# Seven block products instead of eight in more chunks of a MoE layer, behind attention

## The chip, the cores and the metric

The kernel runs on one core of a Trainium2 chip. The metric is the device time of one execution in microseconds (us). Engines are named as in the profile: PE (TensorE: matmuls; PEld its weight loads), DVE (VectorE), ACT (ScalarE), POOL (GpSimd), SP (SyncE, which issues all DMAs here).

## The reference: what is computed

Eight batches of eight heads of causal attention with a decay, 576 tokens and 64 features a head; the result, 4608 tokens of 512 features, goes through a two-layer network (called MoE here, though there is one expert) with 2048 hidden features and the activation mish:

```python
scores = scale * np.matmul(q, k.transpose(0, 1, 3, 2))
decay = cum[:, :, :, None] - cum[:, :, None, :]      # cum: running sum of log(f)
scores = np.where(causal, -1e9, scores + decay)
attn = softmax(scores)                               # over the keys
x = np.matmul(attn, v)                               # -> 4608 x 512
h = x @ w_in                                         # 512 -> 2048
g = h * np.tanh(np.log1p(np.exp(h)))                 # mish
out = g @ w_out                                      # 2048 -> 512
```

All inputs and outputs are float32. The kernel keeps the precision by splitting each float32 operand into two float16 parts, hi and lo, and adding three products: hi·hi, hi·lo and lo·hi.

## The kernel before, in words

**Attention** runs in 32 groups (batch b, pair of heads p; g = 4b + p). A group's queries and keys come in as `qk32`, are split into `hl`, and moved by DMA into `ST1` and `ST2`; scores go to PSUM banks 0 to 3, a DVE pass adds the mask and finds the row's minimum, ACT takes the exponential into `st` (the spare tile `ST1[2]`) or `more_e`, ACT and DVE split it into the two halves of an `hb` tile, and a DMA transpose turns that into `pt` for the product with v (`vv`). The result `x` (tokens on partitions) is split into `xp` and turned by a DMA transpose into `xa`: features on partitions, 512 tokens of one batch in the columns. The last 64 tokens of all batches collect in `xat`.

**The MoE layers** run in nine chunks of 512 tokens: chunk c < 8 is the first 512 tokens of batch c and reads `xa[c % 2]`; chunk 8 is `xat`. The hidden features go in 16 blocks of 128, j = 0 to 15. The first layer (`m1_items`) adds 4 blocks of inputs with 3 products each, 12 matmuls of 128x128 by 128x512, in a PSUM bank; ACT applies mish into a `me` tile; `halves` rounds it to `gh` (ACT or DVE) and takes the rest `gl` (DVE). The second layer (`m2_items`) makes 12 matmuls a block into banks 4 to 7. In chunks 1 to 8 four blocks of the first layer (`GJ = 4`) alternate with the same four of the second; such a half is a phase, and the phases also group the activations, since mish and the exponential need different tables on ACT. Chunk c's work is recorded interleaved with the attention of batch c + 1, so chunks 7 and 8 have no attention left beside them.

**Seven products.** In chunks 7 and 8 seven pairs of feature blocks (`TWINS`) are done as a 2x2 block product in the Winograd form: two feature blocks by two halves of the 512 inputs on the weight's side, two halves of the inputs by two halves of 256 tokens on the other. `diffs_of` builds four sums and differences of weight blocks, `sums_of` four of the chunk's token blocks, in float32 and split into hi and lo again; `m1_seven` makes seven products of 6 matmuls with 256 columns each in place of eight, in three PSUM banks, and puts the results together with adds into `me`.

**Order.** The program records every instruction with the tiles it touches and its cost by a table, and a planner (`Program.schedule`) makes a list schedule forward and backward several times and emits the instructions in the planned order; on the chip each engine then takes its own list in order, with semaphores between the engines. Tiles come from rings (`Ring.tile`): `tag` names the ring, `bufs` its length, and an instruction that writes a ring's tile waits for the last reader of the buffer's former content. `nc.choose` lets the planner pick the engine. Names in the tables below: `b` is a PSUM bank, `mn` a group's row minima, `wall` all weights as hi and lo, `v` and `vv` the values, `cinv` and `gsc` scales.

Of the kernel before, what the change touches and what calls it, by code (L numbers as in the profile page):

```python
# [58 lines left out]
NME = 5  # L59
NOT = 2  # L60
NGH = 10
GJ = 4
NEX = 2
# [19 lines left out]
NQK = 2  # L83
NX = 1
# [26 lines left out]
TB = "2,4,6,8,10,13,16,19"  # L111
# [13 lines left out]
NV = 6  # L125
# [6 lines left out]
PRIO = 200  # L132
C7 = 7
PLAIN = 0
TWINS = [(0, 1), (2, 3), (4, 5), (6, 7), (8, 9), (10, 11), (13, 14)]
# [442 lines left out]
def attn_moe(ctx: ExitStack, tc: tile.TileContext, qk, v, f, w_in, w_out, out):  # L578
# [78 lines left out]
    xat = xa[2]  # L657

# [275 lines left out]
    def load_qk(g):  # L934
        b, p = divmod(g, NP)
        if g in (2, 3):
# [86 lines left out]
    sel = more_e.rearrange("p a n -> p (a n)").bitcast(F16)[:, 0 : 9 * P].rearrange("p (t k) -> p t k", t=9)  # L1023
# [6 lines left out]
    def max_items(g):  # L1030
# [5 lines left out]
        def begin():  # L1036

            s["mx"] = sp.tile([P, 20], F32, name=f"mx{g}", tag="mx", bufs=4)
            nc.gpsimd.memset(s["mx"][:, 0:8:4], -3e38)
# [354 lines left out]
    def x_items(g):  # L1394
# [29 lines left out]
        return [(parts, 60), (turn, 60), (turn_tail, 60)]  # L1424
# [41 lines left out]
    twin_of = {a: b for a, b in TWINS}  # L1466
    diffs, sums = {}, {}
# [4 lines left out]
    def sums_of(c):  # L1472
        t = xa[c % 2] if c < B else xat
        if c < B:
            halves = [flat16(xa[1 - c % 2])[:, 2048 * d : 2048 * d + 2048] for d in range(2)]
            homes = [(x[:, 0:1024], x[:, 1024:2048]) for x in halves]
        else:
            v = sp.tiles["v32"]
            homes = [[v[2 * d + k].bitcast(F16)[:, 0:1024] for k in range(2)] for d in range(2)]
        spare = [x[:, 0:CH] for x in sp.tiles["pt"] + sp.tiles["x32"]]  # L1480
        for d in range(2):
            ga, gb, f1, f2 = spare[4 * d : 4 * d + 4]
            hi, lo = homes[d]
            sums[c, d] = [x.rearrange("p (k n) -> p k n", k=4) for x in (hi, lo)]
            for g, dt in ((ga, d), (gb, d + 2)):
                nc.choose(*([(e, "tensor_tensor", (), dict(out=g, in0=t[:, dt, 0], in1=t[:, dt, 1], op=ALU.add))]
                    for e in ("vector", "gpsimd")))
            n1, n2 = slice(0, 256), slice(256, CH)
            tt = nc.vector.tensor_tensor
            tt(out=f1[:, n1], in0=ga[:, n2], in1=ga[:, n1], op=ALU.subtract)  # L1490
            tt(out=f1[:, n2], in0=gb[:, n2], in1=ga[:, n2], op=ALU.subtract)
            tt(out=f2[:, n1], in0=f1[:, n2], in1=ga[:, n1], op=ALU.add)
            tt(out=f2[:, n2], in0=gb[:, n1], in1=f2[:, n1], op=ALU.subtract)
            split(hi, lo, (f1, f2))

    def split(hi, lo, fs):
        for k, f in enumerate(fs):
            w = slice(CH * k, CH * k + CH)
            nc.choose(*(scaled(hi[:, w], f, None, e) for e in ("scalar", "vector")))
            nc.choose(*(sub(lo[:, w], f, hi[:, w], e) for e in ("vector", "gpsimd")))  # L1500

    def diffs_of(a):
        k = [x for x, _ in TWINS].index(a)
        home = flat16((sp.tiles["qk32"] + sp.tiles["hl"] + ST2 + ST1)[k])
        hi, lo = home[:, 0:1024], home[:, 1024:2048]
        w1, w2 = (wall[:, place[0, j]] for j in (a, twin_of[a]))
        fa, fb = (more_e[:, k] for k in range(2))
        s1, s2 = (x[:, 0:CH] for x in sp.tiles["v32"][4:6])
        diffs[a] = [x.rearrange("p (k n) -> p k n", k=4) for x in (hi, lo)]
        for f, w in ((fa, w1), (fb, w2)):  # L1510
# [363 lines left out]
```

## Time and profile before

| what | value |
|---|---|
| median of 3 runs | 1040.64 us (1037.7 to 1042.4) |
| the profiled execution | 1045.19 us, of which the span from the first to the last instruction is 1043.5 us |
| mean granted PE clock | 0.989 |
| DMA | 140.44 MB, mean 135 GB/s |

The page of a profile gives, for each engine, its busy time, share of the span and number of instructions; then 40 slices of the span, in which a digit is a tenth of busy time (PEclk: of granted clock); then the chain of work that ended last; then groups of equal instructions with their total busy time, the mean of one in ns, and the idle time of the engine just before them with what ended it. Every instruction of the program is recorded through one line of a helper, so the rows have one line number (L311) and are told apart by their tiles: `me<-b,cinv` is the mish that reads a PSUM bank and writes `me`. A matmul's length in the records includes its latency; two in a row overlap, so a rate is read from a run of them.

### The profile page before, as it was taken

The page shows a single profiled execution, that of the slowest core. Times are in us where ns is not written, and L with a number is a line of the kernel's source. Part 1 is how long each engine was busy: PE and PEld are TensorE (multiplying, and loading weights), DVE is VectorE, ACT ScalarE, POOL GpSimd, SP SyncE. Part 2 cuts the span into 40 slices and gives each one's busy share as a digit, 9 for nine tenths or more (in the row PEclk, how much of TensorE's full clock was granted, in tenths as well). Part 3 has the DMA queues.
Part 4 walks back from the last instruction along what each step waited for, and adds up shares of the span by engine and source line. Part 5 has one row for each costly group of instructions (what it writes and reads, how often), then busy time and mean ns, then how long its engine had stood idle before and what let it go on. Part 6 is the DMA issues. An engine that isn't in the chain of part 4 may idle for free.

```text
span 1043.5 us, 20548 instructions
## 1 busy us (share of the span) xinstructions
PE 998.4 (96%) x7638; PEld 557.7 (53%) x7638; DVE 739.6 (71%) x2043; ACT 703.1 (67%) x1309; POOL 13.0 (1%) x73
## 2 busy tenths in 40 slices
PE   2899999999999999999999999999999999999998
PEld 1687565544454544455555445454544545656664
DVE  8777788997777677776766767777676559962432
ACT  6565698987777867776777776778677675443322
POOL 1000001000000000000000000000000000000000
PEclk9898999999999999999999999999999999999999
DMA  7857737399776966776676776766557423001001
GB/s 216 257 177 220 230 92 204 88 212 238 176 144 138 202 135 132 158 163 145 147 148 153 169 148 135 153 158 134 116 125 144 86 56 80 15 4 41 1 1 41
DMA packets 245409, 140.44 MB, mean 135 GB/s; under 512 B 213436, under 2 KB 214012, under 8 KB 245308
## 3 DMA queue, kind: packets, MB, share of 16 engines
q1 hardware_dynamic: 245308, 139.12, 57.7%
q8 instruction: 60, 0.98, 0.4%
q14 instruction: 41, 0.34, 0.1%
HBM read 47.78 MB, written 11.76 MB: 57 GB/s over the span
## 4 chain that ended last, share of the span: by engine, by line
PE 62%; DVE 14%; ACT 10%; DMA 8%; issue 4%; SPq 2%; POOL 0%; ACTq 0%; DVEq 0%; POOLq 0%
PE b L311 62%; DMA qk<-in_qk_dram 2%; DMA pt<-hb 2%; DVE wall L311 2%; SPq L311 2%; DVE b L311 2%; ACT hb L311 2%; DMA st<-hl 2%; ACT st L311 1%; ACT junk L311 1%; ACT more_e L311 1%; DVE hb L311 1%; DVE gl L311 1%; DVE hl L311 1%; DVE x L311 1%
## 5 line engine op out<-in xcount | busy, mean ns | idle before, releaser
L311 PEld LDWEIGHTS <-wall 128*128 128x128 f16 x3372 | 321.3, 98 | 353.6 <-issue 19.7
L311 PE MATMUL b<-gh,wall 128*128 128x512 f16 x1152 | 369.7, 380 | 1.7 <-DVE ot L311 0.9
L311 PE MATMUL b<-xa,wall 128*128 128x512 f16 (+1 forms) x1602 | 344.2, 365 | 5.0 <-ACT me L311 3.5
L311 PE MATMUL b<-gl,wall 128*128 128x512 f16 x576 | 218.5, 379 | 0.0
L311 PE MATMUL b<-st 70*128 70x256 f16 (+10 forms) x978 | 151.4, 288 | 27.1 <-DMA st<-cumd 18.7
L311 PEld LDWEIGHTS <-st 128*128 128x128 f16 (+3 forms) x1170 | 93.9, 104 | 85.0 <-issue 25.6
L311 DVE SCALAR_TENSOR_TENSOR gl<-me,gsc,gh 128x512 f16<-128x512 f32 x144 | 106.4, 748 | 38.9 <-ACT gh L311 37.4
L311 ACT ACTIVATE me<-b,cinv 128x512 f32<-128x512 f32 (+1 forms) x130 | 85.2, 660 | 58.5 <-PE b L311 57.6
L311 PE MATMUL b<-vv,pt 128*128 128x64 f16 (+3 forms) x2492 | 118.8, 208 | 4.4 <-DMA pt<-hb 1.6
L311 ACT ACT_TABLE_LOAD x74 | 94.9, 1283 | 1.5 <-DVE cinv L311 0.2
L311 DVE CUSTOM_DVE_ANT_0 b<-b,mskw 128x512 f32<-128x512 f32 (+2 forms) x150 | 84.8, 566 | 11.6 <-PE b L311 9.2
L311 ACT ACTIVATE more_e<-b,mn 128x512 f32<-128x512 f32 (+3 forms) x114 | 58.8, 539 | 32.6 <-DVE mn L311 30.5
L311 ACT ACTIVATE st<-b,mn 128x512 f32<-128x512 f32 (+3 forms) x111 | 57.5, 547 | 28.9 <-DVE mn L311 26.4
L311 PEld LDWEIGHTS <-pt 128*128 128x128 f16 (+1 forms) x2100 | 64.9, 101 | 19.4 <-DMA pt<-hb 4.0
L311 DVE TENSOR_TENSOR hb<-st,hb 128x512 f16<-128x512 f32 x75 | 51.6, 689 | 29.8 <-ACT hb L311 29.6
L311 DVE TENSOR_TENSOR hb<-more_e,hb 128x512 f16<-128x512 f32 x75 | 51.5, 688 | 28.1 <-ACT hb L311 27.8
L311 ACT ACTIVATE gh<-me,gsc 128x512 f16<-128x512 f32 x84 | 60.1, 719 | 2.0
L311 DVE TENSOR_SCALAR gh<-me,gsc 128x512 f16<-128x512 f32 x60 | 28.9, 484 | 37.2 <-ACT me L311 36.2
L311 ACT ACTIVATE junk<-qk 128x576 bf16<-128x576 f32 x60 | 40.7, 678 | 21.0 <-DMA qk<-in_qk_dram 20.4
L311 ACT ACTIVATE hb<-st 128x512 f16<-128x512 f32 x75 | 46.8, 627 | 8.9 <-DMA pt<-hb 7.2
L311 ACT ACTIVATE hb<-more_e 128x512 f16<-128x512 f32 x75 | 46.8, 626 | 6.4 <-DMA pt<-hb 5.8
L311 DVE TENSOR_SCALAR rr<-b 128x4 f32<-128x4 f32 (+1 forms) x64 | 10.3, 161 | 55.8 <-PE b L311 55.7
(165 smaller groups left out, 1022.4 us busy)
## 6 DMA issues: line engine op xcount, KB each, us to landing
st<-hl SPq DMA_DIRECT2D x180, 144.0 KB
qk<-in_qk_dram SPq DMA_DIRECT2D x30, 576.0 KB
v<-in_v_dram SPq DMA_DIRECT2D x32, 288.0 KB
out_dram<-ot SPq DMA_DIRECT2D x36, 256.0 KB
wall<-in_w_in_dram SPq DMA_DIRECT2D x16, 512.0 KB
wall<-in_w_out_dram SPq DMA_DIRECT2D x16, 512.0 KB
pt<-hb SPq DMA_TRANSPOSE x150
part<-ot SPq DMA_DIRECT2D x8, 256.0 KB
```

The lines of the kernel that those rows point to most:

```text
L311: r = getattr(real[eng], method)(*a, **kw)
```

## The change

More pairs are done with seven products. `pairs_of` gives the pairs by their first block: chunks 2 to 6 now have 4, 6, 8, 10 (`MID`), chunk 7 has 4, 6, 8, 10, 12, 14, chunk 8 all eight. Blocks 12 and 13, 14 and 15 are pairs in place of 13 and 14.

- The contraction is split into blocks 0, 2 and 1, 3 instead of 0, 1 and 2, 3.
- `totals` builds the token sums for chunks 2 to 7 from the attention's `x` of two groups, ahead of its splitting: 4 DVE operations of 256 columns into two `ot` tiles, split into `hb`, and turned by DMA transposes into a new tile `tw` (four for a chunk's two halves). `x32` has two buffers for it. `tail_totals` does it for chunk 8.
- `diffs_of` builds the weights' sums. For the middle pairs it runs in chunk 1, ahead of blocks 12 to 15 (`DJ = 12`), into a new tile `dw`; for the others at the start of chunks 7 and 8. It takes all four `me` tiles as scratch. The sum of the second block's two halves is written over one of that block's halves in `wall`, which is not needed alone any more.
- `m1_seven` uses two PSUM banks, both halves of each, and puts the results together in PSUM: three copies of a half bank into `me` tiles, three adds from a half bank and a copy back into a half bank, and one mish of 512 columns for each of the two blocks.
- Rings: `me` 5 to 4, `gh` and `gl` 10 to 7, `more_e` 2 to 1, `qk32` 2 to 1, `v32` 6 to 4 (so a batch's v is loaded two groups later), `mx` 4 to 3, `x32` 1 to 2. One qk load goes into `tw`. A limit in the weights' steps (`TB`) goes from 13 to 14.

The constants and the loop around it:

```diff
-NME = 5
+NME = 4
-NGH = 10
+NGH = 7
-NEX = 2
+NEX = 1
-NQK = 2
-NX = 1
+NQK = 1
+NX = 2
-NV = 6
+NV = 4
-PLAIN = 0
-TWINS = [(0, 1), (2, 3), (4, 5), (6, 7), (8, 9), (10, 11), (13, 14)]
+TWINS = [(0, 1), (2, 3), (4, 5), (6, 7), (8, 9), (10, 11), (12, 13), (14, 15)]
+MID = [4, 6, 8, 10]
+LAST = [0, 2, 12, 14]
+C0 = 2
+DJ = 12
+PLAIN = 4
...
+    pairs_of = {c: MID if C0 <= c < C7 else [] for c in range(NCHUNK)}
+    pairs_of[C7] = MID + [a for a in LAST if a >= PLAIN]
+    pairs_of[B] = MID + LAST
...
+            if c == C0 - 1 and j0 == DJ:
+                for a in MID:
+                    w0(lambda a=a: diffs_of(a))
```

The token sums, and what a pair does now in place of three banks and six adds into `me`:

```diff
+    def four_totals(f1, f2, x, y):
+        tt = nc.vector.tensor_tensor
+        tt(out=f1[:, N1], in0=x[:, N2], in1=x[:, N1], op=ALU.subtract)
+        tt(out=f1[:, N2], in0=y[:, N2], in1=x[:, N2], op=ALU.subtract)
+        tt(out=f2[:, N1], in0=f1[:, N2], in1=x[:, N1], op=ALU.add)
+        tt(out=f2[:, N2], in0=y[:, N1], in1=f2[:, N1], op=ALU.subtract)
...
+            for k, f in enumerate((f1, f2)):
+                t = sp.tile([P, 2, CH], F16, name=f"tx{k}{g}", tag="hb", bufs=NHB)
+                nc.choose(*(scaled(t[:, 0], f, None, e) for e in SV))
+                nc.choose(*(sub(t[:, 1], f, t[:, 0], e) for e in LW_))
+                nc.sync.dma_start_transpose(
...
-            pa, pb, pc = (psum((3 * k + i) % 4)[:, n1] for i in range(3))
+            pa, pb = (psum((2 - 2 * k + i) % 4) for i in range(2))
...
+            product(a1, weight(a, 0), value(0, N1), True)
+            product(b1, e2, total(2), True)
+            copy(p1, a1)
+            add(b1, b1, p1)
+            product(a2, e1, total(0))
+            product(a1, weight(a, 1), value(1, N1))
+            copy(p5, a2)
+            copy(u2, b1)
+            add(a2, a2, u2)
+            product(b1, e3, total(1))
+            add(b2, b1, p5)
+            product(b1, weight(j, 1), total(3))
+            product(a2, e4, value(1, N2))
+            for i, h, u in ((a, pa, us[0]), (j, pb, us[1])):
+                nc.scalar.activation(out=u, in_=h, func=AF.Mish, scale=cinv[c][:, i : i + 1])
                 halves(c, i, u, CH)
```

The planner sets the order anew. Three places of it follow; in each the first list is of the kernel before and the second of the changed one, and what stands in brackets is what the instruction waits for (`DMAHW` is a transfer).

The first is DVE in chunk 2, in the phase with blocks 8 to 11 (`ISA` is the pass that adds the mask and finds the row minima):

```order
L311 TENSOR_TENSOR hb_194<-more_e,hb_194 128x512 [waits DMAHW4_49,DVE_49,Activation_49]
L311 TENSOR_TENSOR hb_193<-more_e,hb_193 128x512 [waits DMAHW5_49,DVE_49,Activation_49]
L311 TENSOR_SCALAR rr_147<-b_0_118 128x4 [waits PE_49]
L311 RECIPROCAL rr_147<-rr_147 128x4 [waits DVE_49]
L311 ISA b_0_127,mn_200<-b_0_127,mskw 128x512 [waits PE_49]
L311 ISA mn_200 128x1
L311 TENSOR_SCALAR gh_163<-me_162,gsc_101 128x512 [waits Activation_49]
```

```order
L315 TENSOR_TENSOR hb_186<-st_2_84,hb_186 128x512 [waits DMAHW2_49,Activation_49]
L315 TENSOR_TENSOR b_0_119<-b_0_119,me_169 128x256 [waits PE_49]
L315 TENSOR_TENSOR hb_185<-more_e,hb_185 128x512 [waits DMAHW3_49,Activation_49]
L315 TENSOR_TENSOR b_0_122<-b_0_122,me_163 128x256 [waits Activation_49]
L315 TENSOR_TENSOR b_0_128<-b_0_128,me_172 128x256 [waits Activation_49]
L315 TENSOR_TENSOR b_0_121<-b_0_121,me_166 128x256 [waits PE_49,Activation_49]
L315 TENSOR_TENSOR b_0_122<-b_0_122,me_163 128x256 [waits PE_49]
L315 TENSOR_TENSOR b_0_119<-b_0_119,me_169 128x256 [waits PE_49]
L315 TENSOR_TENSOR hb_186<-st_2_84,hb_186 128x512 [waits DMAHW0_49,DVE_49,Activation_49]
```

Six adds in PSUM, of two pairs that run interleaved, came in among the attention's subtractions.

The second is ACT at the same place:

```order
L311 ACTIVATE hb_193<-more_e 128x512
L311 ACT_TABLE_LOAD
L311 ACTIVATE me_162<-b_0_120,cinv_97 128x512
L311 ACTIVATE me_165<-b_0_121,cinv_97 128x512
L311 ACTIVATE gh_166<-me_165,gsc_101 128x512
```

```order
L315 ACTIVATE me_169<-b_0_128 128x256 [waits PE_49]
L315 ACTIVATE hb_186<-st_2_84 128x512 [waits DMAHW2_49]
L315 ACTIVATE hb_185<-more_e 128x512 [waits DMAHW3_49,Activation_49]
L315 ACTIVATE me_163<-b_0_121 128x256 [waits PE_49]
L315 ACTIVATE me_163<-b_0_121 128x256
L315 ACTIVATE me_172<-b_0_119 128x256 [waits DVE_49]
L315 ACTIVATE me_169<-b_0_128 128x256 [waits PE_49]
L315 ACTIVATE me_166<-b_0_122 128x256 [waits DVE_49]
L315 ACTIVATE hb_186<-st_2_84 128x512 [waits DMAHW0_49,Activation_49]
L315 ACT_TABLE_LOAD [waits DVE_49,PE_49]
```

Six copies of half a bank stand ahead of the mish, among the roundings into `hb`.

The third is DVE in chunk 1, between the `gl` of block 11 and that of block 12:

```order
L311 RECIPROCAL rr_158<-rr_158 128x4 [waits DVE_49]
L311 ISA b_0_127,mn_200<-b_0_127,mskw 128x512 [waits PE_49]
L311 ISA mn_200 128x1
L311 TENSOR_SCALAR gh_188<-me_171,gsc_101 128x512 [waits Activation_49]
L311 TENSOR_TENSOR x_0_148<-b_0_118,rr_158 128x4x64 [waits DVE_49]
```

```order
L315 TENSOR_TENSOR me_166<-wall 128x512
L315 TENSOR_TENSOR me_163<-wall 128x512
L315 TENSOR_TENSOR me_169<-me_166 128x256 [waits DVE_49]
L315 TENSOR_TENSOR dw<-me_172,dw 128x256
L315 TENSOR_TENSOR me_172<-me_169,me_163 128x256 [waits DVE_49]
L315 ISA b_0_121,mn_191<-b_0_121,mskb 128x128 [waits Activation_49]
L315 ISA mn_191 128x1
L315 TENSOR_TENSOR me_169<-me_163,me_166 128x256
L315 TENSOR_TENSOR me_172<-me_163,me_172 128x256 [waits DVE_49]
L315 TENSOR_TENSOR wall<-me_169,wall 128x2x128 [waits Activation_49]
```

The weight differences of the four middle pairs, 40 DVE instructions in all, came in here; these rows are the end of the second pair and most of the third.

More of the change, by code (lines that the diff above doesn't have):

```diff
@@ L110 @@
 GR = [int(x) for x in ("4", "10", "16",)]
-TB = "2,4,6,8,10,13,16,19"
+TB = "2,4,6,8,10,14,16,19"
 NHB = 2
@@ L1422, in turn_tail, with totals @@
                 nc.choose(*(scaled(to[r], both[r, :, r], None, e) for e in CT))
-        return [(parts, 60), (turn, 60), (turn_tail, 60)]
+        def totals(g):
+            c, p = divmod(g, NP)
+            assert ended.get(c - 1, 0) == len(pairs_of[c - 1])
+            xs = [st[k]["x"].rearrange("p t d -> p (t d)") for k in (g - 1, g)]
+            f1, f2 = (sp.tile([P, CH], F32, name=f"tf{i}{g}", tag="ot", bufs=NOT) for i in range(2))
+            four_totals(f1, f2, *xs)
+            for k, f in enumerate((f1, f2)):
[3 more added lines that the diff above has]
+                nc.sync.dma_start_transpose(
+                    out=tw[:, p // 2, k].rearrange("p h (t n) -> p (h t) n", n=P),
+                    in_=t.rearrange("p h (t n) -> p (h t) n", n=P))
+        before = [(lambda: totals(g - 1), 60)] if p == 2 and b >= C0 else []
+        behind = [(lambda: totals(g), 60)] if p == 3 and b >= C0 else []
+        return before, [(parts, 60), (turn, 60), (turn_tail, 60)] + behind
     oacc = {}
@@ L1480, in sums_of, with joined, split, tail_totals @@
+    def joined(out, hi, lo):
+        nc.choose(*([(e, "tensor_tensor", (), dict(out=out, in0=hi, in1=lo, op=ALU.add))]
+            for e in ("vector", "gpsimd")))
+    def split(hi, lo, f):
+        nc.choose(*(scaled(hi, f, None, e) for e in ("scalar", "vector")))
+        nc.choose(*(sub(lo, f, hi, e) for e in ("vector", "gpsimd")))
+    def tail_totals():
+        v = sp.tiles["v32"]
         spare = [x[:, 0:CH] for x in sp.tiles["pt"] + sp.tiles["x32"]]
         for d in range(2):
+            homes = [v[2 * d + k].bitcast(F16)[:, 0:1024].rearrange("p (h n) -> p h n", h=2) for k in range(2)]
+            totals8[d] = homes
@@ L1482, in sums_of @@
             ga, gb, f1, f2 = spare[4 * d : 4 * d + 4]
[L1483 to L1500, printed above, removed]
@@ L1502, in diffs_of @@
[L1502 to L1519 removed]
+            for x, dt in ((ga, 2 * d), (gb, 2 * d + 1)):
+                joined(x, xat[:, dt, 0], xat[:, dt, 1])
@@ L1661, in slot @@
         if "pv" in what and 0 <= t - 2 < NG:
-            groups.append(leading(t - 2, (pv_items if t - 2 < NB else new_pv_items)(t - 2) + x_items(t - 2)))
+            before, behind = x_items(t - 2)
+            groups.append(leading(t - 2, before + (pv_items if t - 2 < NB else new_pv_items)(t - 2) + behind))
         if ahead:
```

128 lines of the change are left out of this document (63 added, 65 removed).

## The prediction

> **What bounds the kernel now.** I read the busy times and slices of the page first, then the chain of waits, then the stages one by one.
>
> ```profile
> PE 998.4 (96%) x7638; PEld 557.7 (53%) x7638; DVE 739.6 (71%) x2043; ACT 703.1 (67%) x1309; POOL 13.0 (1%) x73
> PEclk9898999999999999999999999999999999999999
> PE 62%; DVE 14%; ACT 10%; DMA 8%; issue 4%; SPq 2%; POOL 0%; ACTq 0%; DVEq 0%; POOLq 0%
> ```
>
> TensorE (PE) is busy 96% of the span and holds 62% of the chain that ended last. The stages, from the busy times of stretches (columns: stretch, then busy us and count of PE, PEld, DVE, ACT, POOL, then granted clock, DMA share, GB/s), tell where it is dense:
>
> ```profile
> 50.00:100.00 50.00, 48.11 (x480) 40.39 (x477) 35.95 (x113) 30.55 (x71) 0.58 (x4) 0.90 0.65 177
> 100.00:150.00 50.00, 48.13 (x311) 28.54 (x310) 41.56 (x119) 37.65 (x74) 0.11 (x1) 0.93 0.60 179
> 150.00:200.00 50.00, 48.83 (x315) 29.68 (x315) 41.99 (x117) 44.48 (x77) 5.10 (x12) 1.00 0.54 144
> 200.00:250.00 50.00, 48.93 (x346) 24.21 (x345) 46.70 (x142) 43.19 (x74) 0.14 (x1) 1.00 0.93 209
> 250.00:300.00 50.00, 47.55 (x376) 23.85 (x375) 37.73 (x122) 38.06 (x78) 0.28 (x2) 1.00 0.83 188
> 300.00:800.00 500.00, 491.93 (x3941) 250.53 (x3939) 356.96 (x1020) 368.94 (x686) 2.63 (x19) 1.00 0.69 147
> ...
> 875.00:900.00 25.00, 24.55 (x161) 15.40 (x159) 25.00 (x57) 13.67 (x25) 0.00 (x0) 1.00 0.17 53
> 900.00:960.00 60.00, 60.00 (x378) 36.72 (x377) 36.52 (x78) 24.67 (x44) 0.00 (x0) 1.00 0.01 2
> ```
>
> From 300 to 800 us, where chunks 2 to 6 run beside the attention, PE is busy 98.4%, DVE 71% and ACT 74%. So a matmul that goes away there shortens the span, as long as DVE and ACT keep delivering. The last two rows are chunk 7 (879 to 960 us), which already has pairs with seven products: beside its first pairs DVE is full and PE loses 0.45 us in 25, then PE loses nothing.
>
> **The change part by part.** *Products.* Pairs with seven products go from 7 + 7 = 14 (chunks 7, 8) to 4 in each of chunks 2 to 6, 6 in chunk 7 and 8 in chunk 8: 34, so 20 more. A plain pair is 24 matmuls of 512 columns, a pair of seven is 42 of 256. In the order 480 matmuls of 512 columns go and 840 of 256 come. Their rate, from the timeline (start, length, engine, group):
>
> ```profile
> 614.53 10.52 PE L311 MATMUL b<-xa,wall 128*128 128x512 f16 x48
> 599.71 0.38 PE L311 MATMUL b<-xa,wall 128*128 128x512 f16 x1
> 965.85 1.47 PE L311 MATMUL b<-v,qk 128*128 128x256 f16 x12
> 965.74 0.27 PE L311 MATMUL b<-xa,wall 128*128 128x256 f16 x1
> ```
>
> 48 in a row less the length of one: (10.52 - 0.38) / 47 = 0.216 us each. At 256 columns: (1.47 - 0.27) / 11 = 0.109 us. A pair costs 24 x 0.216 = 5.18 us or 42 x 0.109 = 4.58 us. The gain is 0.6 us a pair, **20 x 0.6 = -12.0 us**, all of it on PE.
>
> *What DVE and ACT get for it.* The nearest rows (busy, mean ns of one):
>
> ```profile
> L311 DVE TENSOR_TENSOR me<-b,hb 128x256 f32<-128x256 f32 x42 | 17.4, 421 | 36.9 <-PE b L311 36.5 <-ACT me L311 0.4
> L311 ACT ACTIVATE hb<-b 128x256 f32<-128x256 f32 x14 | 5.2, 380 | 21.3 <-PE b L311 21.3
> L311 DVE TENSOR_TENSOR pt<-pt,pt 128x256 f32<-128x256 f32 x8 | 3.2, 418 | 0.0
> L311 DVE TENSOR_TENSOR hb<-st,hb 128x512 f16<-128x512 f32 x75 | 51.6, 689 | 29.8 <-ACT hb L311 29.6
> L311 ACT ACTIVATE hb<-st 128x512 f16<-128x512 f32 x75 | 46.8, 627 | 8.9 <-DMA pt<-hb 7.2 <-DVE gl L311 1.0
> L311 DVE TENSOR_TENSOR more_e<-wall 128x512 f32<-128x512 f16 x14 | 9.5, 681 | 0.0
> ```
>
> A pair now has 3 adds in PSUM (0.42 each, DVE) and 3 copies out of PSUM (0.38 each; the order gives 85 of 102 to ACT). A chunk has 4 pairs, and the totals of two halves: 8 subtractions or adds of 256 columns, 4 rounded halves (mostly ACT), 4 rests (DVE, 0.69). DVE: 12 x 0.42 + 2 x 0.42 + 8 x 0.42 + 4 x 0.69 + 1.2 x 0.5 (roundings that fall to DVE, an estimate between the 0.42 and 0.69) = 12.6 us. ACT: 10 x 0.38 + 2.8 x 0.63 = 5.6 us. How long a chunk is:
>
> ```profile
> L311 PE MATMUL b<-gh,wall 128*128 128x512 f16 x244 | 80.4, 380 | 0.0
> L311 PE MATMUL b<-gl,wall 128*128 128x512 f16 x122 | 46.3, 379 | 0.0
> ```
>
> These are the second layer's matmuls in 550 to 750 us: 366, where a chunk has 192, so 105 us a chunk. DVE has 0.714 x 105 = 75 us in it now, ACT 77. After, DVE has 88 of about 103 us (85%) and ACT 83 (81%). The stretch 200 to 250 us shows DVE at 93% and ACT at 86% with PE still at 98%, so this load as such is covered.
>
> *Weight differences.* For the four middle pairs they are built ahead of features 12 to 15 of chunk 1, at about 210 to 240 us. A pair takes DVE 2 x 0.68 + 4 x 0.42 + 4 x 0.42 = 4.7 us, four pairs 18.9. They use all four `me` buffers, and the activations of features 12 to 15 wait behind them for a buffer; behind those wait PE's next two banks. DVE's idle time between 200 and 300 us is 100 - 46.7 - 37.7 = 15.6 us. With the totals of chunk 2 (6.1) and its first two pairs' adds (2.5) the new work is 27.5 us. Lower end 0: the work spreads to both sides, and PE has 48 second-layer matmuls and attention to go on with. Upper end 27.5 - 15.6 = 11.9 us. I take **+3**, a quarter, because DVE is still 29% idle right behind it.
>
> *The chain inside a pair.* Three banks per pair became two, and sums are made in PSUM: the third product of a chain cannot start before a copy, an add and another copy are done. The rows for one link, in chunk 8 now:
>
> ```profile
> 960.61 0.82 PE L311 MATMUL b<-xa,wall 128*128 128x256 f16 x6
> 961.46 0.38 ACT L311 ACTIVATE hb<-b 128x256 f32<-128x256 f32 x1 [1.26 <-PE b L311]
> 962.19 0.42 DVE L311 TENSOR_TENSOR me<-b,hb 128x256 f32<-128x256 f32 x1 [8.01 <-PE b L311]
> 962.57 0.49 PE L311 MATMUL b<-xa,wall 128*128 128x256 f16 x3
> ```
>
> The product's last matmul ends at 961.43 and the copy starts 0.03 us later: an idle engine answers at once. In the new order two pairs are interleaved, so PE has the other pair's products (0.65 us each) to cover add and copy. Both engines take their queue in order, though: DVE meets its second add behind a subtraction into `hb` that waits for a transfer, and six copies stand on ACT with only short gaps. Lower end 0 (900:960 lost nothing, at DVE 61%). Upper end one copy and one add bare per pair, 0.38 + 0.42 = 0.8 us, 16 us in all. I take 0.15 a pair, **+3**: nearer to the lower end, by the row 875:900, where two pairs ran beside a full DVE and PE lost 0.45 us, but with ACT at 55%, where it is at 74% in the middle.
>
> *Moved loads and rings.* One qk buffer, four v buffers (v is loaded two groups later), seven `gh`/`gl`, one `more_e`, two x, and 24 more transposes on SP's queue.
>
> ```profile
> ACT junk L311 <- DMA qk<-in_qk_dram: 20.4, 15, 2.7
> ACT junk L311 <- DMA v<-in_v_dram: 5.6, 5, 2.9
> ACT hb L311 <- DMA pt<-hb: 13.0, 20, 1.4
> L311 SPq DMA_TRANSPOSE pt<-hb x150: 1231/1278/2885, 197.8 to 868.4; - x150
> ```
>
> 24 x 1.28 = 31 us of SP's queue; DMA is at 69% there. The `hb` ring costs ACT 13.0 / 150 = 0.09 us a use, so 24 to 48 more uses cost 2 to 4 us of ACT time, off PE. ACT's waits for qk and v (26 us) are not on PE's path now: DVE and attention are a group ahead. If this cover went, the five waits for v (5.6 us) would be the price. In the other direction, the start is reshuffled, and PE's idle time in the three stretches from 50 to 200 us, 1.9 + 1.9 + 1.2 = 5 us, is the most that a better one could give there. Ends -5 and +5.6, taken **0**.
>
> Sum: -12.0 + 3 + 3 + 0 = **-6.0 us**. The profiled execution took 1045.19 us (span 1043.5 and 1.7 around it), so it would be 1039.2; the median of the runs, 1040.64, lies 4.6 lower, so **1034.6 us**. What the pairs in chunks 7 and 8 exchange (6 for 7, 8 for 7) is in the 20.
>
> [...] The two halves of a pair's sum now share a bank. [...]
>
> **The rivals.** *All of it is covered.* For it: chunk 7 and the row 200:250. Against: in chunk 7 no attention stands beside the pairs. 1040.6 - 12.0 = 1028.6 us.
>
> *DVE becomes the bound.* Its 88 us a chunk are a mean; the half chunk with the pairs and totals has more of it. For it: 250:300, where PE is at 95% while DVE has only 75%, so waits appear before DVE is full.
>
> ```profile
> 282.17 1.59 PE L311 MATMUL b<-vv,pt 128*128 128x65 f16 x54 [1.33 <-DMA pt<-hb]
> PE b L311 <- ACT me L311: 3.5, 5, 1.3
> ```
>
> Single waits of PE are already up to 1.33 us; one or two more per pair phase, 10 phases, make about 9, and with the differences' 3 the gain is gone: 1040.6 us.
>
> [...]
>
> That the matmuls are not removed is excluded by their count in the order.
>
> **How the numbers follow.** Forecast (1031 to 1038.5) 0.38; all covered 0.22; DVE the bound 0.23; banks 0.17. The range, 1025 to 1046, reaches the first two rivals, with a part of the start's -5, and a part of the last; the forecast's own is 1031 to 1038.5. A change under 0.5% (5.2 us) cannot be told from none. Faster: 0.22 + 0.6 of 0.38 + 0.03 = 0.48. Same: 0.4 of 0.38 + 0.17 + 0.02 = 0.34. Slower: 0.18, from the last two.
>
> **What would show it.** Right: the 256-column matmuls in chunks 2 to 6 keep 0.109 us, PE stays above 97% in 300 to 780 us, waits of PE for `b` or `me` from DVE and ACT total 3 to 5 us more, DVE shows 83 to 87%. The differences show as a PE gap at 215 to 235 us behind `me`. Wrong: PE at 95% or less with waits behind DVE adds (the bound or the banks), or a start (to 200 us) that moved by more than 4 us.

## The result, and the profile after

The changed kernel takes 1054.1 us (1052.5 to 1056.7 in four runs) against 1040.6, a ratio of 1.0135 [1.0104, 1.0166]: slower, outside the predicted range. The profiled execution took 1056.7 us with a span of 1055.0. The busy times and the slices of the granted clock on its page:

```profile
PE 999.3 (95%) x8000; PEld 600.0 (57%) x8000; DVE 777.7 (74%) x2183; ACT 733.3 (70%) x1406; POOL 13.3 (1%) x73
PEclk9679999999999999999999999999999999999999
```

PE has 362 instructions more (480 long matmuls went, 840 short ones came, and two small ones), and is busy as long as before. Two things are to be seen: the clock is lower in the second and third slice (6 and 7, where 8 and 9 stood; before, the fourth slice had an 8 too), and in the middle PE now waits. The stretches of the profile before in which the clock was low:

```profile
24.00:40.00 16.00, 10.95 (x103) 7.96 (x102) 13.47 (x35) 7.98 (x20) 0.10 (x1) 0.79 0.94 290
72.00:88.00 16.00, 14.85 (x97) 11.36 (x97) 11.92 (x38) 11.96 (x27) 0.11 (x1) 0.68 0.52 125
100.00:112.00 12.00, 10.72 (x74) 7.07 (x73) 7.97 (x22) 5.82 (x14) 0.00 (x0) 0.72 0.63 196
```

and those of the changed kernel, with the middle (the columns are those of the prediction: PE, PEld, DVE, ACT, POOL, granted clock, DMA share, GB/s):

```profile
24.00:40.00 16.00, 11.52 (x102) 8.58 (x102) 13.32 (x36) 9.96 (x27) 0.10 (x1) 0.68 0.93 302
40.00:64.00 24.00, 21.77 (x130) 18.57 (x131) 16.86 (x52) 10.61 (x26) 0.35 (x2) 0.57 0.62 203
...
100.00:112.00 12.00, 9.93 (x69) 8.16 (x68) 10.76 (x30) 6.51 (x15) 0.00 (x0) 0.72 0.75 204
256.00:268.00 12.00, 9.12 (x87) 5.36 (x85) 8.44 (x23) 6.42 (x11) 0.14 (x1) 0.72 0.57 151
300.00:800.00 500.00, 482.38 (x4125) 275.15 (x4123) 396.57 (x1155) 390.02 (x754) 2.49 (x18) 1.00 0.78 157
```

Length times the missing share of the clock gives the time lost to it: 3.4 + 5.1 + 3.4 = 11.9 us before, 5.1 + 10.3 + 3.4 + 3.4 = 22.2 after. From 300 to 800 us the clock is full, and PE is busy 482.4 of 500 us where it was 491.9. What it waits for between 300 and 880 us, before:

```profile
PE b L311 <- ACT me L311: 2.8, 3, 1.3
PE b L311 <- DVE x L311: 2.0, 2, 1.4
PE b L311 <- ACT st L311: 1.3, 5, 0.4
PE b L311 <- ACT more_e L311: 1.2, 4, 0.4
PE b L311 <- DVE mn L311: 0.9, 1, 0.9
```

and in the changed kernel (us in total, times, longest):

```profile
PE b L315 <- ACT me L315: 7.1, 11, 1.6
PE b L315 <- ACT st L315: 4.4, 8, 1.4
PE b L315 <- DVE x L315: 2.7, 3, 1.6
PE b L315 <- ACT more_e L315: 1.3, 2, 0.8
PE b L315 <- DVE me L315: 0.5, 1, 0.5
```

8.2 us became 16.0 in these rows, most of it behind ACT. These rows hide part of each wait, since a matmul's recorded length includes its latency (0.38 us are recorded for one of 512 columns, where in a row one starts every 0.216 us). So the text below uses a second reading of the same trace, called **loss**: from each matmul's start to the next one's start, less what its columns take at the full rate (0.216 us for 512, 0.109 for 256, 0.03 for up to 70), summed over a stretch (differences under about 0.01 us are left out). It also counts a low clock. The parts of the two profiled executions by this reading:

| | before | after | difference |
|---|---|---|---|
| PE's own work at full rate | 940.4 | 928.5 | -11.9 |
| loss to 300 us (with the low clock) | 75.1 | 82.4 | +7.3 |
| loss from 300 to 880 us (clock full) | 24.3 | 39.3 | +15.0 |
| loss behind 880 us | 1.0 | 2.4 | +1.4 |
| span | 1043.5 | 1055.0 | +11.5 |

(Read the last column: the four differences make 11.8, and the time before the first matmul and from the start of the last one on, 23.1 and 22.7 us, takes off 0.4. The two other columns do not add up to the span: with those 23 us they come out 20 us too high, in both kernels alike, because many short matmuls start closer together than their rate here says. The expectations of e1 to e8 use a slightly coarser threshold, on which the middle lost 23.0 and 37.8.) Since every run lists its span and mean clock, a run's lost clock is span x (1 - clock). The medians: before 9.4 us (83 runs beside the experiments, median 1042.4 us), after 20.0. What is left, the time at full clock, is 1031.9 us before and 1031.8 after. This takes off too much, though: over the 83 runs of the kernel before, a run is longer by only 0.67 us for each us of lost clock. By that slope, an estimate, the 10.6 us more of lost clock make about 7 of the 11.7 us between the medians 1042.4 and 1054.1; the table gives 3.1 us more for the middle (15.0 against 11.9) and 1.4 for the end. **So the 12 us of matmuls that went away were paid for by 15 us of waits in the middle, and most of the slowdown that is measured in this order goes with the lower clock of the first 300 us.**

### The profile page after: what moved, and what is told of

The parts are those of the page before. It is cut to its first block, busy times and chain, and to the rows that moved or that the text cites. A ratio compares the mean times of both kernels' runs of the same rounds, so it can differ in the third digit from the quotient of the medians.

```text
span 1055.0 us, 21676 instructions
## 1 busy us (share of the span) xinstructions
PE 999.3 (95%) x8000; PEld 600.0 (57%) x8000; DVE 777.7 (74%) x2183; ACT 733.3 (70%) x1406; POOL 13.3 (1%) x73
## 5 line engine op out<-in xcount | busy, mean ns | idle before, releaser
L315 PE MATMUL b<-xa,wall 128*128 128x512 f16 (+1 forms) x1320 | 265.7, 346 | 10.1 <-ACT me L315 5.8
L315 PE MATMUL b<-st 70*128 70x128 f16 (+12 forms) x978 | 154.5, 288 | 26.8 <-DMA st<-cumd 18.6
L315 ACT ACTIVATE me<-b,cinv 128x512 f32<-128x512 f32 x144 | 95.3, 683 | 35.5 <-PE b L315 34.2
L315 ACT ACTIVATE st<-b,mn 128x512 f32<-128x512 f32 (+3 forms) x150 | 77.6, 543 | 29.4 <-DVE mn L315 26.4
L315 DVE TENSOR_TENSOR b<-b,me 128x256 f32<-128x256 f32 x102 | 41.7, 428 | 70.0 <-PE b L315 56.6
L315 DVE CUSTOM_DVE_ANT_0 b<-b,mskw 128x256 f32<-128x256 f32 (+2 forms) x150 | 84.1, 562 | 12.3 <-PE b L315 8.9
L315 ACT ACTIVATE me<-b 128x256 f32<-128x256 f32 x85 | 31.6, 381 | 67.3 <-PE b L315 58.1
L315 PEld LDWEIGHTS <-pt 128*128 128x128 f16 (+1 forms) x2100 | 65.9, 102 | 21.2 <-issue 7.3
L315 PEld LDWEIGHTS <-dw 128*128 128x128 f16 (+1 forms) x624 | 60.2, 100 | 15.9 <-issue 6.1
L315 ACT ACTIVATE more_e<-b,mn 128x384 f32<-128x384 f32 (+2 forms) x75 | 39.0, 543 | 29.8 <-DVE mn L315 28.6
L315 PEld LDWEIGHTS b<-vv,pt 128*128 128x128 f32 x392 | 50.9, 206 | 3.7 <-issue 0.8
```

Of the source, the lines that this page charges most:

```text
L315: r = getattr(real[eng], method)(*a, **kw)
```

## The experiments

Each ran beside the kernel before, and the ratios are to it. All numbers in one place; "loss" is that from 300 to 880 us of the profiled execution, "waits" the part of it in gaps over 60 ns which another engine or a DMA ended, "lost clock" and "at full clock" (the span less all lost clock, so a lower bound) are medians of the runs:

| kernel | median us | ratio | lost clock | at full clock | loss | waits |
|---|---|---|---|---|---|---|
| before | 1042.4 | 1 | 9.4 | 1031.9 | 24.3 | 11.0 |
| after | 1054.1 | 1.0135 [1.0104, 1.0166] | 20.0 | 1031.8 | 39.3 | 25.6 |
| e1 no pairs in chunks 2 to 6 | 1043.9 | 1.0029 [0.9998, 1.0059] | 8.9 | 1033.2 | 24.4 | 12.1 |
| e3 after, answer times 250/260 | 1042.9 | 0.9994 [0.9964, 1.0024] | 5.7 | 1034.3 | 34.9 | 19.9 |
| e4 before, shorter rings | 1054.1 | 1.0111 [1.0053, 1.0169] | 12.1 | 1038.1 | 25.0 | 12.1 |
| e5 no sums in pairs | 1046.2 | 1.0061 [1.0035, 1.0086] | 17.7 | 1026.4 | 30.1 | 16.8 |
| e6 before, 250/260 | 1038.1 | 0.9983 [0.9958, 1.0007] | 10.9 | 1025.9 | 20.1 | 6.9 |
| e7 after, other order | 1063.1 | 1.0235 [1.0197, 1.0273] | 18.0 | 1044.5 | 44.7 | 24.8 |
| e8 before, other order | 1051.5 | 1.0117 [1.0084, 1.0150] | 8.9 | 1040.3 | 30.2 | 7.1 |
| e9 totals once | 1058.2 | 1.0155 [1.0122, 1.0187] | 19.1 | 1037.7 | 42.0 | 26.6 |
| e10 no sums, totals once | 1038.5 | 0.9962 [0.9947, 0.9977] | 13.0 | 1023.9 | 26.0 | 13.7 |
| e11 sums first | 1054.2 | 1.0109 [1.0075, 1.0142] | 11.6 | 1041.3 | 45.4 | 28.0 |
| e12 copies on DVE | 1051.4 | 1.0094 [1.0060, 1.0129] | 12.1 | 1037.3 | 38.7 | 24.8 |
| f1 sums behind the pair | 1048.4 | 1.0054 [1.0026, 1.0081] | 9.9 | 1034.5 | 38.2 | 24.7 |
| f2 one pair in a group | 1065.9 | 1.0199 [1.0154, 1.0245] | 10.6 | 1052.4 | 50.9 | 31.9 |
| f3 the same, 250/260 | 1063.6 | 1.0191 [1.0159, 1.0223] | 6.9 | 1053.1 | 44.6 | 30.0 |
| f4 two pairs a chunk, 250/260 | 1056.8 | 1.0136 [1.0110, 1.0161] | 9.5 | 1045.8 | 39.6 | 25.2 |
| f5 sums in SBUF | 1050.8 | 1.0063 [1.0032, 1.0095] | 15.7 | 1032.5 | 33.3 | 20.2 |
| f6 before, 350/360 | 1038.1 | 0.9957 [0.9942, 0.9972] | 8.3 | 1028.1 | 21.2 | 7.9 |
| f7 after, 350/360 | 1047.9 | 1.0055 [1.0034, 1.0077] | 11.5 | 1035.3 | 33.9 | 17.8 |

How much too low "at full clock" can be is seen in e6: its three runs at a clock of 0.998 took 1035.9 to 1037.2 us, its five at 0.985 to 0.987 took 1037.5 to 1041.3, so 12 us more of lost clock cost 2.7 by the medians. And in e9, e11 and f2 the clock was not full in the middle: one, two and three spells of 3.4 us at half clock make 1.7, 3.4 and 5.1 us of their loss. The two of e11:

```profile
397.30:400.60 3.30, 3.30 (x9) 1.06 (x7) 2.75 (x7) 3.27 (x9) 0.00 (x0) 0.50 0.56 105
574.80:578.10 3.30, 2.88 (x7) 1.01 (x7) 2.86 (x7) 2.30 (x4) 0.00 (x0) 0.50 0.88 228
```

### Where the time is lost

**e1: the changed kernel without pairs in chunks 2 to 6.** The rings, the form of a pair in chunks 7 and 8 and the pairs there stay.

```diff
-C0 = 2
+C0 = 7
```

> The changed kernel with its first chunk of middle pairs set from 2 to 7 (C0 = 7): chunks 2 to 6 run plain pairs, no token sums are made for them, the weight differences move to chunk 6. The shorter rings and the form with two banks stay. PE work is 14 pairs of seven, as before. Theory 1 (the chain inside the middle pairs is late: copies and adds do not come in time): the loss goes with the pairs, 1041 to 1045 us. Theory 2 (the shorter rings, above all one qk buffer, make loads and ACT late everywhere): the loss stays and the 12 us of PE work come back, 1055 to 1066 us. Theory 3 (the added DVE and ACT work of sums and differences as such): about 1041 to 1045, as theory 1.

Its loss is that of the kernel before in both parts, 75.1 us to 300 and 24.4 from there. So shorter rings and the new form cost nothing to speak of in this order, and the 15 us belong to the pairs in the middle, with the totals made for them.

**e4: the kernel before with the changed rings.** Where the kernel before keeps things in the rings that are now shorter, small tiles take their place.

```diff
-NME = 5
+NME = 4
-NQK = 2
+NQK = 1
...
```

> The kernel before with the changed kernel's ring lengths (me 4, gh and gl 7, more_e 1, qk32 1, x32 2, v32 4, mx 3; the weight differences' scratch in me tiles, the selection matrix in a tile of its own) and nothing else. Theory 1 and 3: within 4 us of before, 1037 to 1045. Theory 2: 1050 to 1058 us.

With one `qk` buffer and no other home for it, group 1's load went over group 0's queries and keys, so group 0 computes scores of other data; the work is the same. The profiled execution (1046.4 us) and the three other runs (1053.8 to 1056.7) differ by 7 to 10 us, and only 1 to 6 of them are lost clock. The median lies in the range named for the rings, while e1, with the same rings, took 1043.9. Its loss in the middle, 25.0, says what e1 says; on the start e4 settles nothing.

### Is it one unlucky order?

The planner lays out the whole program anew at every edit. Three pairs of runs change the order alone, in both kernels.

**e3, e6: longer answer times.** The planner's allowance from the end of a DVE or ACT instruction to what waits for it:

```diff
-    DELAY = {"tensor": 197, "vector": 140, "scalar": 150, "gpsimd": 80}
+    DELAY = {"tensor": 197, "vector": 250, "scalar": 260, "gpsimd": 80}
```

> The changed kernel with one number changed in the planner: the delay from the end of a DVE or ACT instruction to its reader from 140 and 150 ns to 250 and 260, so that it leaves about 0.11 us more for each link of a chain. Theory 1 (links planned too short): 1043 to 1049 us. Theory 2 and 3: 1050 to 1057, the order changes but not what is short.

> The kernel before, unchanged in what it computes, but ordered with the longer answer times that brought the changed kernel from 1054 to 1043 us (VectorE 250 instead of 140 ns, ScalarE 260 instead of 150). Chain theory: the pairs' links were what these answer times helped, and the kernel before has hardly any: 1038 to 1044 us, loss from 300 to 880 us 20 to 25 us. General theory (longer answer times are better for every part): 1036 us or less, loss 18 or less. Order theory: the first 300 us come out otherwise by chance, 1034 to 1050 us, with the clock.

**e7, e8: slightly shuffled first ranks.**

```diff
-NZ = 0
+NZ = 40
-SEED = 122
+SEED = 7
```

> The changed kernel with the same work, ordered from slightly shuffled first ranks (noise of 40 on them, one seed), so that only the order of instructions differs. Chain theory: the loss from 300 to 880 us stays at 34 to 42 us, since every order is made with the same short answer times, and the time is 1046 to 1058 us, by the clock alone. Order theory: loss and clock both move; a time of 1046 us or less, or a loss of 30 or less, would show that the 13 us were one bad order.

> The kernel before with the same work, ordered from the same shuffled first ranks. Chain theory: loss from 300 to 880 us 20 to 26 us and the time within 4 us of 1041. Order theory: the time differs from 1041 by more than 5 us, and the clock of the first 300 us goes with it (lost clock 12.5 us before).

**f6, f7: still longer answer times,** 350 and 360.

> The kernel before, unchanged in what it computes, ordered with answer times of 350 and 360 ns (140 and 150 in the kernel before; 250 and 260 gave a ratio of 0.998). If longer answer times help in general: 1032 to 1037 us, loss from 300 to 880 us 16 to 20 us. If 1038 was one order among many: 1038 to 1050.

> The changed kernel ordered with answer times of 350 and 360 ns. If links planned too short cost the 15 us, loss goes on falling: 39.3 at 140, 34.9 at 250, then 29 to 32, time 1034 to 1040, faster than both kernels. If the sums cost whatever the plan allows for them: loss 33 to 40, time 1040 to 1050.

An order alone moves the kernel before from 1038.1 to 1051.5 us and the changed one from 1042.9 to 1063.1, and e7 and e8 lie outside what the chain theory gave them in time and in loss. At first e3 looked like proof of links planned too short: 11 us gained. It was not: its loss in the middle fell by 4.4 us, that of the kernel before by 4.2 (e6), and its lost clock fell from 20.0 to 5.7 us, which is more than the rest of the gain. What does not move is the difference between the kernels in the middle, order by order: 39.3 - 24.3 = 15.0, 44.7 - 30.2 = 14.5, 34.9 - 20.1 = 14.8, 33.9 - 21.2 = 12.7 us. As measured, the changed kernel is slower in each of the four orders, by 11.7, 11.7, 4.8 and 9.8 us; with all lost clock taken off it is 0.1 us faster, then 4.2, 8.4 and 7.2 slower. So the middle's price is the change's own, 0.64 to 0.75 us for each of the 20 pairs, above the 0.6 that a pair saves; that alone makes 1 to 3 us of each difference, and the rest arises outside the middle. f7 shows that a looser plan does not take the price away. The clock, on the other hand, goes with the order: 10.6 and 9.1 us more, then 5.2 less, then 3.2 more.

f6, like e6, is faster than both kernels with nothing changed but that allowance; its middle, before's being in the prediction:

```profile
300.00:800.00 500.00, 495.40 (x3965) 252.60 (x3964) 352.73 (x1027) 374.28 (x702) 2.62 (x19) 1.00 0.71 148
```

### What in the pairs costs it

**e5: no sums.** The three copies and three adds of a pair are left out, the last product goes to a half bank of its own; the first layer's values are not the reference's.

```diff
-            copy(p1, a1)
-            add(b1, b1, p1)
...
-            copy(p5, a2)
-            copy(u2, b1)
-            add(a2, a2, u2)
...
-            add(b2, b1, p5)
-            product(b1, weight(j, 1), total(3))
+            product(b2, weight(j, 1), total(3))
```

> The changed kernel, but its pairs of seven lack their three copies out of PSUM and three additions in PSUM (the last product goes into a half bank of its own), so the first layer's values are not the reference's; all 42 matmuls, the totals, the weight differences and the buffers stay. Loss below is the time between starts of matmuls beyond their own issue rate, from 300 to 880 us, where the clock is full: 23.0 us before, 37.8 in the changed kernel. Chain theory (products wait for copies and additions): the loss falls to 26 us or less, the time by 10 us or more, to 1044 or less. Load theory (totals, roundings and their transposes crowd DVE and ACT): the loss stays at 34 us or more, the time at 1050 or more. Order theory (a new order of the whole program moves the stalls of the first 300 us, whatever the edit): the loss from 300 us on says nothing about it; the granted clock of the span moves between 0.978 and 0.997 and the time with it.

(e2, the same but with the last product left where it was, leaves half a bank without a value and gave no time.) The loss fell by 9.2, to 30.1 us: between the two numbers named. The time fell 8 us although the clock stayed nearly as bad. What PE waits for in the middle, to be read against the changed kernel's 7.1 and 4.4:

```profile
PE b L315 <- ACT me L315: 3.8, 6, 1.1
PE b L315 <- ACT st L315: 2.0, 4, 0.8
PE b L315 <- ACT more_e L315: 1.6, 4, 0.5
```

The waits that shrank are mostly those behind ACT's mish and attention's evictions, which are no sums: of the 7.1, one wait of 1.0 us ended with a copy of half a bank, the rest with a mish. By starts of matmuls, some 3.5 us of the changed kernel's 25.6 us of waits end with a copy or an add of a pair. But these are single orders, and orders alone move the loss by 10 us (20.1 to 30.2 before, 33.9 to 44.7 changed), more than this 9.2.

**e9, e10: totals for chunk 2 alone,** with and without sums. Chunks 3 to 6 use chunk 2's totals, so their values are not the reference's.

```diff
         def totals(g):
             c, p = divmod(g, NP)
+            if c > C0:
+                return
```

> The changed kernel, but the totals of the input chunks are made for chunk 2 alone and used in chunks 3 to 6 too, so the first layer's values there are not the reference's; all matmuls, copies and additions of the pairs stay. Gone: in four chunks 8 subtractions and additions, 4 roundings, 4 rests and 4 transposes each. Loss is PE's time beyond its issue rate between 300 and 880 us, on the scale where the kernel before lost 24.3 us, the changed one 39.3, the changed one without copies and additions in its pairs 30.1. Theory that the rest of 5.8 us over before is the totals: the loss falls by 4 to 7 us, to 32 to 35. Theory that the copies and additions cost all and the 5.8 are a matter of order: it stays at 38 to 41. Theory that DVE's load decides (totals are more DVE time than the additions): it falls by more than 9, to 30 or less.

> The changed kernel without the copies and additions in its pairs and with totals made for chunk 2 alone (its first layer's values are not the reference's); its matmuls are all there. If sums and totals are the whole cost of the new pairs, the loss from 300 to 880 us is that of the kernel before, 22 to 27 us on the same scale. If there is a cost of their own in the narrower products or the shorter rings, it stays at 30 or more. Time: 1050 less what the granted clock gives back; with the clock of the kernel before (0.99) and a loss of 24, 1031 to 1036 us.

With the sums in place the totals are worth nothing (42.0, of which 1.7 is the clock's); without sums 4.1 us (26.0). With both away the middle loses what the kernel before loses, within 1.7 us: the products of 256 columns and the rings have no price there that one order can show. Even this kernel, with the sums and most totals left out, took 1038.5 us, 4 less than before, where 12 us of matmuls are gone; its lost clock is 13.0 where it was 9.4.

**e11: sums first.** Copies and adds stand 3 us further forward in rank.

```diff
             def add(o, x, y):
+                nc.lead = 3000.0
                 nc.vector.tensor_tensor(out=o, in0=x, in1=y, op=ALU.add)
+                nc.lead = 0.0
```

> The changed kernel, complete, whose copies and additions inside the pairs stand 3 us further forward in the rank by which VectorE and ScalarE choose their next instruction. If the products wait because these sums stand behind attention's work in the queues: loss from 300 to 880 us falls from 39.3 to 33 or less, time to 1048 or less. If it is the other way round, attention's evictions and activations wait behind the sums (the waits in the changed kernel's trace stand mostly behind ScalarE's evictions of scores and its activations), the loss stays or grows: 39 to 46, time 1052 to 1062.

**e12: all copies on DVE.**

```diff
-                nc.choose(*(scaled(o, x, None, e) for e in ("scalar", "vector")))
+                nc.choose(scaled(o, x, None, "vector"))
```

> The changed kernel, complete, with all 102 copies out of PSUM on VectorE instead of 85 on ScalarE: ScalarE loses some 32 us of work in the span, VectorE gains some 36. If ScalarE's queue is where PE's time goes (its evictions stand behind the copies): loss from 300 to 880 us 30 to 35, time 1044 to 1050. If VectorE is the engine near its bound: loss 42 to 50, time 1056 to 1066. If only the length of the chain counts (copy and addition take 0.38 and 0.42 us on either engine): 37 to 42.

Served first, the sums cost no less: 45.4, or 42.0 without the 3.4 of the clock, against 39.3. That is the second of its two expectations, and fits other work standing behind them. A copy of half a bank takes 0.38 us on ACT and 0.42 on DVE in the changed kernel's trace (85 and 17 of them), an add 0.43 on DVE. Which engine copies makes no difference that one order can show (38.7); ACT's queue alone is not the cause.

**f1: the same six sums, all behind the pair's last product.** No product waits for a sum any more; the first layer's values are not the reference's.

```diff
+            product(b1, weight(j, 1), total(3))
+            product(a2, e4, value(1, N2))
+            copy(p1, a1)
+            add(b1, b1, p1)
+            copy(p5, a2)
+            copy(u2, b1)
+            add(a2, a2, u2)
+            add(b2, b1, p5)
```

> The changed kernel whose pairs make the same three copies and three additions, but all six behind their last product instead of between the products (the first layer's values are not the reference's; the load of VectorE and ScalarE is the same, and the matmuls too). Scale: loss of PE from 300 to 880 us, 24.3 in the kernel before, 39.3 in the changed one, 30.1 without copies and additions. If the products' wait inside the pair is what the sums cost (chain): 29 to 34 us, time 1044 to 1049. If the load of the two queues is (attention's evictions and the activations stand behind the sums): 37 to 43 us, time 1051 to 1057. A bank held by an access would be spread over both; the sums now hold the two banks at the pair's end, 2.4 us longer, so above 43 would say that the release of the banks decides.

The loss stayed at 38.2 us, as the load theory had it; the time, 1048.4, fell into the chain theory's range, with 9.9 us of lost clock where it was 20.0. Waits ahead of the pairs' own products fell from 8.4 to 3.9 us, and those ahead of other matmuls rose by 3.6. In its rows the place of a wait changed, not the sum:

```profile
PE b L315 <- ACT me L315: 6.4, 9, 1.5
PE b L315 <- DVE x L315: 2.7, 4, 1.3
PE b L315 <- ACT st L315: 2.4, 7, 0.7
PE b L315 <- DVE mn L315: 1.3, 1, 1.3
```

So the wait of a product inside its pair, on which the chain term rested, is not what the 15 us are made of: taken away, it comes back at the next bank or the next group of attention.

**f5: six instructions of the same size, in SBUF alone,** ahead of the mish as before; no product waits for them and they touch no bank (values are not the reference's).

```diff
-            copy(p1, a1)
-            add(b1, b1, p1)
+            sv = us[1][:, N2]
+            copy(p1, sv)
+            add(p5, sv, sv)
...
```

> The changed kernel whose pairs make three copies and three additions of the same size, but from one buffer in SBUF into the pair's other buffers there, with no operand in PSUM (the first layer's values are not the reference's); the two engines have the same number of instructions more, ahead of the pair's activations as in the changed kernel, but no product waits for them and they hold no bank. Scale: loss of PE from 300 to 880 us 24.3 before, 39.3 in the changed kernel, 38.2 with all sums behind the pair, 30.1 without sums. If the load of the two queues is what costs: 36 to 42 us. If it is that the sums stand between products, banks and activations: 28 to 33 us.

33.3 us, just above the second case: 3.2 above no sums, 6.0 below the real ones (1.3 of it is one gap that begins at 299.7 us and ends behind 300).

```profile
PE b L315 <- ACT me L315: 5.1, 6, 1.5
PE b L315 <- ACT st L315: 4.6, 9, 1.1
PE b L315 <- ACT gh L315: 0.9, 1, 0.9
```

Read as a ladder, the waits go 11.0 (before), 13.7 (pairs without sums and with old totals), 16.8 (totals in each chunk), 20.2 (sums' load in SBUF), 24.7 (sums in PSUM, behind the pair), 25.6 (between the products). Each step is no larger than what orders move in one kernel (6.9 to 11.0 before, 17.8 to 25.6 after), so only the ends are settled: six kernels without middle pairs wait 6.9 to 12.1 us, eleven kernels with sums in the middle 17.8 to 31.9; their losses, 20.1 to 30.2 and 33.9 to 50.9, do not overlap either. Whether the last 5 us are the banks that are held or the activation that waits for the sums was not told apart.

**f2, f3, f4: fewer pairs, each with plain features as cover.**

```diff
-MID = [4, 6, 8, 10]
-LAST = [0, 2, 12, 14]
+MID = [2, 6, 10]
+LAST = [0, 4, 8, 12]
```

> The changed kernel with three pairs a chunk instead of four in chunks 2 to 6, each with two plain features beside it in its group of four (feature blocks 2, 6 and 10 with their neighbours), 5 pairs in chunk 7 and 7 in chunk 8; 27 pairs in all where the changed kernel has 34, the same values. PE's own work: 13 pairs more than before, -7.8 us. If a pair's sums cost because the only other products in their group are those of a second pair with sums of its own (chain without cover): the loss falls to 25 to 30 us and the time to 1035 to 1043. If each pair has its price whatever stands beside it (0.75 us): 24.3 + 11 = 35 us, time 1043 to 1050.

> The same with three pairs a chunk, ordered with the longer answer times (250 and 260 ns). Scale for this ordering: the kernel before 20.1 us of loss from 300 to 880 us and 1038.1 us, the changed one 34.9 and 1042.9. Chain without cover: loss 20 to 25 us, time 1030 to 1036, faster than both kernels. A price for each pair: loss 31 us, time 1040 to 1043.

In f4, `pairs_of` gives blocks 4 and 8 alone in chunks 2 to 6:

```diff
-    pairs_of = {c: MID if C0 <= c < C7 else [] for c in range(NCHUNK)}
+    pairs_of = {c: [4, 8] if C0 <= c < C7 else [] for c in range(NCHUNK)}
```

> Ordered with the longer answer times, two pairs a chunk in chunks 2 to 6 (blocks 4 and 8), each alone in its group of four; chunks 7 and 8 as in the changed kernel: 24 pairs, 10 more than before, PE's own work -6.0 us; the values are the same. Scale: before 20.1 us of loss and 1038.1 us with these answer times. Chain without cover: loss 20 to 24 us, time 1032 to 1036. A price of 0.75 us for each pair: loss 27.6 us, time 1038 to 1041.

(Against what was written, f4's values are not the reference's: blocks 7 and 11 run plain in the middle with weights over which differences were written. Its work is as described.) Both theories miss by far: 50.9 (45.8 without the clock's part), 44.6 and 39.6 us of loss with 15, 15 and 10 pairs in the middle. f2 shows one reason, since its first pair now stands at the start of a chunk and needs totals that are still under way (of the 7.7 us in the first row, 3.7 end with copies of half banks):

```profile
PE b L315 <- ACT me L315: 7.7, 11, 2.1
PE b L315 <- DMA tw<-hb: 3.4, 3, 1.7
PE b L315 <- ACT st L315: 3.0, 7, 0.9
```

f4 loses 39.6 with 10 pairs, where the changed kernel with the same answer times loses 34.9 with 20. So "a price for each pair" does not hold either: mixed groups cost more per pair than groups of two pairs. Why is open.

## Why the prediction was wrong, step by step

- **Products, -12.0:** right. At these rates they make -11.9, and from 300 to 800 us the matmuls of 256 columns follow one another at 0.109 us, as in chunk 8.
- **The load of DVE and ACT, "covered":** the sizes were high, not low: DVE is busy 79% from 300 to 800 us, ACT 78%, where 85 and 81 were worked out. That it is therefore covered was the wrong inference. The stretch 200 to 250 us, from which it was taken (93% with PE at 98%), shows that the engines can be fuller without loss in one place; f5 and e10 put some 3 us for the sums and 4 for the totals down to load alone, at 79%, so far as single orders tell. What the added work cost here did not follow from the share of time that was left.
- **Weight differences, +3 at 215 to 235 us:** wrong in place, and worth 0. The planner put them at 305 to 338 us, where PE lost 1.0 us (1.5 before); most of that stretch:

```profile
305.00:330.00 25.00, 25.00 (x207) 13.02 (x206) 24.90 (x70) 19.50 (x42) 0.14 (x1) 1.00 0.64 124
```

- **The chain inside a pair, "+3", 0.15 us a pair:** this is the step that failed. In four orders the 20 pairs cost PE 12.7 to 15.0 us in the middle, 0.64 to 0.75 us each; in one order each, the sums are 9 us of it (e5) and the totals 4 more (e10). The upper end, 0.8, was right; the choice between the ends was not. It was made by the row 875:900, two pairs beside a full DVE, but without attention; the sign that was passed over is that in the middle attention's evictions and mish stand in the same two queues. The mechanism was off too: it is not mainly the products behind a sum that wait (f1; 3.5 of 25.6 us of waits end with a copy or an add) but other work's matmuls. That they wait because that work stands behind the sums in the queues fits e11, f1 and f5, but is not proven against the banks that the sums hold.
- **Moved loads and rings, 0, ends -5 to +5.6:** e1 confirms 0 for the rings as such. In this order the first 300 us still lost 7.3 us more, beyond the end, while the clock, which was no term of the sum, lost 10.3 us more there; apart from the clock the start became 3 us shorter. PE's longest gap between 50 and 300 us is one that a ring explains (one `qk` buffer: ACT waits for its load, DVE for ACT, PE for DVE; start, length, instruction, idle before):

```profile
253.39 0.68 ACT L315 ACTIVATE junk<-qk 128x576 bf16<-128x576 f32 x1 [3.26 <-DMA qk<-in_qk_dram]
255.01 0.17 DVE L315 TENSOR_SCALAR qa<-qa 128x2 f32<-128x2 f32 x1 [3.59 <-ACT junk L315]
...
259.34 2.60 PE L315 MATMUL b<-vv,pt 128*128 128x65 f16 x54 [2.88 <-DVE x L315]
...
263.00 1.06 PE L315 MATMUL b<-gh,wall 128*128 128x512 f16 x2
```

  The two matmuls of 512 columns at 263.00 take 1.06 us where 0.60 is usual: the granted clock is 0.50 from 258.50 to 265.30.
- **The clock, no term:** of the 19.5 us between the forecast 1034.6 and the measured 1054.1, the middle makes 9.0 (15.0 where +3 and +3 had been set), and about 7 go with the clock by the estimate above. The prediction's own rows from 50 to 150 us had it at 0.90 and 0.93. That this order drew a worse clock is chance as far as the runs tell: e3, the same work, lost 5.7 us to it.
- **The rivals:** "all covered" fell; "DVE becomes the bound" fell, as DVE has more room than was thought. The "banks" of the chances (0.17) stands for the idea that a copy or an add in one half of a bank keeps PE out of its other half. No run shows such a lock: of PE's 25.6 us of waits 3.5 end with a copy or an add of a pair, the rest with other work, and f5, whose six instructions touch no bank, lost 6.0 us less than the changed kernel, in one order, which is all that is left for the banks.
- **What would show it:** PE at 96.5% in the middle lay between the two marks (97 and 95), its waits rose by 7.8 us in the rows above, where 3 to 5 had been named for a right forecast, and the start moved by more than 4 us (by 112 us the clock alone had lost 18.8 us where it was 11.9), which had been named as the sign of a wrong forecast.

## What to carry to other kernels

Here DVE and ACT were 79% and 78% busy in the middle, and the work added to them was not covered: PE lost 12.7 to 15.0 us more there. So work added to two queues that also evict another stage's banks should not be priced by the idle share; ask what stands behind it in the queues, and take the price from a place where that other stage runs. When a planner lays the program out anew, run both versions in several orders before believing a difference of one per cent, and read the stretch that the edit touches separately from the start. Note the granted clock of each run: here 10.6 us more were lost to it, for which the edit had no term.

## What the runs showed of the chip

Lost clock came in pieces. In the stretches above PE ran at half clock for 6.8, 10.2 and 6.8 us before, and for 10.2, 20.5, 6.8 and 6.8 us after: multiples of 3.4 us, each 1.7 us of lost clock. The last of these spells, 6.8 us long, began during PE's gap of 2.88 us that ends at 259.34. The second and the last of those after:

```profile
43.45:63.92 20.47, 20.47 (x119) 17.79 (x118) 13.58 (x42) 9.74 (x24) 0.35 (x2) 0.50 0.56 192
258.50:265.30 6.80, 5.96 (x68) 3.79 (x68) 4.46 (x13) 3.00 (x5) 0.14 (x1) 0.50 0.36 96
```

In e3 a gap of nearly the same length, 2.84 us, was followed by none:

```profile
27.39 0.27 PE L315 MATMUL b<-st 128*128 128x128 f16 x1 [2.84 <-DMA st<-cumd]
```

```profile
24.00:40.00 16.00, 11.83 (x98) 8.51 (x97) 12.02 (x36) 9.30 (x23) 0.10 (x1) 1.00 0.91 296
```

In each of the 20 traces all spells at half clock start on one grid of 3.413 us. Those of the changed kernel in its first 300 us start at 26.38, 43.45, 101.48 and 258.49 us, which are 5, 17 and 46 steps of the grid apart. But where a gap falls on the grid does not explain the two cases. In the changed kernel 2.03 us of the gap lie in the step from 255.08 to 258.49, and half clock followed; in e3 1.96 us of the gap, and 0.77 us of a gap before it, lie in the step from 23.09 to 26.51, and none followed. Why is open. One kernel's runs differ by their clock as well: over 83 runs of the kernel before it is 0.988 to 0.997, and the run's time goes with the clock lost (correlation 0.86).
